# Two ends of the on-chip memory swapped, and y of the second MoE put on the weights' remainder

## The chip, the cores and the metric

One core of one Trainium2 chip runs the whole program. The metric is the device time of one execution in microseconds (us); the time before is the median of three runs.

## The reference

Inputs are q, k, v of shape (4, 8, 576, 64) and a decay f, and the weights of two pairs of dense layers. What is computed is

```python
scores = q @ k.T / sqrt(64) + decay(f)          # causal, per batch and head
x = softmax(scores) @ v                         # 2304 tokens x 512
x = leaky(x @ w_in) @ w_out                     # first MoE,  512 -> 2048 -> 512
out = ((x @ w_a) * (x @ w_b)) @ w_out2          # second MoE, 512 -> 1536 -> 512
```

All three parts run in full float32 accuracy: an operand is split into a high and a low part of type float32r, and each product is made of three matmuls (high by high, high by low, low by high).

## The kernel before, in words

The program is one function, scheduled by a list scheduler in the order in which it is written; it places the waits itself. TensorE does all products. A matmul has a stationary operand (first loaded as weights, 128 x 128) and a moving operand, which streams past it; in the profile `ab<-yh,wa_hi` means that the moving yh met the stationary wa_hi.

- **Attention** goes in eight blocks (`att_steps`, L642), all its tiles in the pool `att` (L136). P is transposed by TensorE against the identity: the identity moves (it lies in `cpool`), p is stationary.
- **First MoE**: nine chunks of 256 tokens (i) by sixteen slices of the hidden width (fi). `work` (L688) issues `l1` (L529: 12 matmuls L537, stationary w_in, moving x, 256 columns) and, two or three steps later, `l2` (L551: 12 matmuls L559, stationary w_out, moving gh and gl, 256 columns). x, hs, gh and gl lie in the pool `moe_a` (L130), every third x in `late` (L718). Raw weights come through the pool `stage` (L132), go by ScalarE, VectorE and GpSimd into float32r (`load_weight`, L105) and stay in `wpool` (L58), 64 tiles of 2048 bytes per partition. Attention blocks are interleaved up to chunk 6. y goes to device memory (L569).
- **Second MoE**: five blocks n of 512 tokens (the last has 256) by twelve slices fi. `l3` (L598) issues 24 matmuls L608 (stationary w_a, w_b; moving yh, yl; 512 columns, in the last block 256), and `l4` (L622) issues for each of 4 groups of tokens (2 in the last block) 3 matmuls L631 (stationary ph or pl, moving w_out2, 512 columns). `load_y` (L587) brings y back and splits it, for block 0 before and for block n + 1 at fi = 4 of block n: the y of even blocks lies in the pool `wx`, that of odd blocks in `wk` (L589). `wx` (L733) also holds ph, pl, the raw weights and eight weight tiles: both parts of w_a, w_b and w_out2 of fi = 0 and of w_a of fi = 1 (L581); the other weights take over `wpool`, tile by tile, as the first MoE lets go of them. `wx` opens when `att` has closed, `wk` when `moe_a` has closed (L745 to L747).

A pool is a stretch of each partition. Pools are stacked from the bottom upwards, or, with side="right", from the top (byte 229344) downwards. A place is told here by its first byte in the partition; it follows from the pools' sizes, in the order in which they open. In the kernel before:

```
cpool   1152 ..   2240     identity at 1152
wpool   2240 .. 133312     64 weight tiles of 2048
moe_a 133312 .. 158912     xh, xl, hs, gh, gl      (later wk, 133312 .. 153792: yh, yl, os)
stage 158912 .. 172224     raw weights             (later late, 158912 .. 167104: xh, xl)
att   172704 .. 229344     attention               (later wx, 167904 .. 229344: 8 weight tiles,
                           raw, yh at 200672, yl at 208864, p, ph and pl from 221152)
```

All these tiles are multiples of 64 bytes long but for some small ones of attention, which lie at multiples of 32, so the remainder of a tile's place by 64 is mostly that of its pool: 0 for cpool's identity, wpool, moe_a, wk, stage and late, 32 for att and wx. By 512 it is 192 for wpool, moe_a and wk, and 480 for wx's weights, y, ph and pl.

Of the kernel before, what the change touches and what calls it, by code (L numbers as in the profile page):

```python
# [9 lines left out]
F32R = mybir.dt.float32r  # L10
# [4 lines left out]
PSUM = bass.MemoryType.PSUM  # L15
DRAM = bass.MemoryType.DRAM

P = 128
# [8 lines left out]
def kernel(  # L27
# [19 lines left out]
    NF1, NF2, ND = F1 // P, F2 // P, DM // P  # L47
# [37 lines left out]
    def split(hi, lo, src, lo_engine=None):  # L85

        nc.scalar.copy(hi, src)  # L87
        (lo_engine or nc.gpsimd).tensor_tensor(out=lo, in0=src, in1=f32(hi), op=ALU.subtract)
# [38 lines left out]


    moe_ctx = ExitStack()
    mp = moe_ctx.enter_context(tc.tile_pool(name="moe_a", bufs=2))  # L130
    stage_ctx = ExitStack()
    stage = stage_ctx.enter_context(tc.tile_pool(name="stage", bufs=2))  # L132
    late = {}
    ps_y = moe_ctx.enter_context(tc.tile_pool(name="ps_y", bufs=2, space=PSUM))
    att_ctx = ExitStack()
    ap_ = att_ctx.enter_context(tc.tile_pool(name="att", bufs=1, side="right"))  # L136
    ps_a = att_ctx.enter_context(tc.tile_pool(name="ps_att", bufs=1, space=PSUM, side="right"))


# [10 lines left out]
    for t in range(5):  # L150
        n = min(P, S - t * P)
# [357 lines left out]
    def att_tail(b):  # L509

        tok0 = b * S + 512
        c = tok0 // T1
        c0 = tok0 - c * T1
        ch, cl = x_chunk(c)
        pp = ps_a.tile([P, HP, 64], F32, tag="ps", bufs=3, name=f"ppx_{b}")
        for hp in range(HP):
            pe_att.transpose(pp[:, hp, :], x4[b][0:64, hp, :], ident[:64, :64])
        evac(ch[:, :, c0 : c0 + 64], cl[:, :, c0 : c0 + 64], pp)
# [53 lines left out]
    T2 = 512  # L572
    blocks2 = [(t, min(T2, NT - t)) for t in range(0, NT, T2)]
    wb = {}
    right = ExitStack()
    pools = {}

    def load_b(fi):
# [8 lines left out]
    def load_y(n):  # L587
        t0, tn = blocks2[n]
        pool = pools["wk" if n % 2 else "wx"]  # L589
        yh = pool.tile([P, ND, T2], F32R, tag="yh", bufs=1, name=f"yh_{n}")  # L590
        yl = pool.tile([P, ND, T2], F32R, tag="yl", bufs=1, name=f"yl_{n}")
        for d in range(ND):
            t = pools["wx"].tile([P, T2], F32, tag="t", bufs=2, name=f"sy_{n}_{d}")[:, :tn]
            nc.sync.dma_start(t, y_dram[d, :, t0 : t0 + tn])
            split(yh[:, d, :tn], yl[:, d, :tn], t, nc.vector if n == 0 else None)
        yb[n] = (yh, yl)
# [118 lines left out]
    for item in one[:8]:  # L715
        work(*item)
    stage_ctx.close()
    late["p"] = moe_ctx.enter_context(tc.tile_pool(name="late", bufs=1))  # L718
    att_tail(0)
    for _ in att_steps(2):  # L720
        pass
# [8 lines left out]
                if i % 2 == 0:  # L730
                    att_tail(i // 2)
    att_ctx.close()
    pools["wx"] = right.enter_context(tc.tile_pool(name="wx", bufs=2, side="right"))  # L733
    pools["ps_ab"] = right.enter_context(tc.tile_pool(name="ps_ab", bufs=2, space=PSUM, side="right"))

    for fi in range(NF1):
        for i in (NB1 - 2, NB1 - 1):
            work(i, fi)
        if fi == 11:
            load_y(0)  # L740
        while len(wb) < NF2 and 4 * fi >= 6 * (len(wb) + 1) - 8:
            load_b(len(wb))
# [1 line left out]
        l2(*pend.pop(0))  # L744
    moe_ctx.close()  # L745
    wk_ctx = ExitStack()
    pools["wk"] = wk_ctx.enter_context(tc.tile_pool(name="wk", bufs=2))  # L747
    pools["ps_o"] = wk_ctx.enter_context(tc.tile_pool(name="ps_o", bufs=4, space=PSUM))
    while len(wb) < NF2:
        load_b(len(wb))  # L750
# [1 line left out]
    for n in range(len(blocks2)):  # L752
        for fi in range(NF2):
            pend.append((n, fi, *l3(n, fi)))
            if fi == 4 and n + 1 < len(blocks2):
                load_y(n + 1)
            if len(pend) > 1:
                l4(*pend.pop(0))
    while pend:
        l4(*pend.pop(0))  # L760
    wk_ctx.close()
    right.close()


# [28 lines left out]
```

## Time and profile before

| what | value |
|---|---|
| median of 3 runs | 1154.49 us (1154.03 to 1155.28) |
| the profiled execution's own time | 1155.12 us |
| its span, first to last instruction | 1153.3 us |
| granted TensorE clock, mean | 0.995 |

The profile is of one execution. Its views used below are the page (busy time of engines, the chain that ended last, DMA issues), the busy time by stretches of the span, the chain of waits in order of time (each piece: start, length, what it is, and how many instructions were merged; the length of a piece of matmuls divided by their count is the spacing from one matmul's start to the next), the timeline of an engine, and SyncE's waits. A matmul's own duration in the trace is a latency and not the spacing: matmuls overlap.

### The profile page before, as it was taken

How to read it: one execution, taken by the hardware profiler on the slowest of the kernel's cores; microseconds unless marked ns; L12 is line 12 of the kernel's file. 1: busy time of each engine (PE TensorE's matmuls, PEld its weight loads, DVE VectorE, ACT ScalarE, POOL GpSimd, SP SyncE). 2: the span in 40 equal slices, each digit the busy share in tenths (PEclk: the TensorE clock that was granted, in tenths of full speed). 3: DMA queues.
4: the chain of work that ended last, by engine and by line, in shares of the span. 5: the costliest groups of instructions: out<-in, count | busy, mean ns of one | idle time of the engine just before them, and what ended most of it. 6: DMA issues, size and time to landing. Idle time of an engine off the chain costs nothing.

```text
span 1153.3 us, 20360 instructions
## 1 busy us (share of the span) xinstructions
PE 1112.6 (96%) x7021; PEld 981.9 (85%) x7021; DVE 658.0 (57%) x1780; ACT 571.8 (50%) x1511; POOL 286.8 (25%) x486
## 2 busy tenths in 40 slices
PE   6999989999999999999999899999999999999998
PEld 3677778999989999999999887888888888888897
DVE  6789998887878787866459978111111211211122
ACT  5557687888877777867445545212111211211121
POOL 5556553333233323322124324101000100100000
PEclk9999999999999999999999999999999999999999
DMA  7556645433353234521234444101000100100010
GB/s 195 162 150 171 149 121 107 91 79 63 66 122 77 55 69 95 104 51 30 88 115 129 149 143 145 40 1 55 19 1 1 64 1 1 39 8 1 1 37 19
DMA packets 188583, 86.82 MB, mean 75 GB/s; under 512 B 144640, under 2 KB 174336, under 8 KB 188480
## 3 DMA queue, kind: packets, MB, share of 16 engines
q1 hardware_dynamic: 183296, 80.80, 27.9%
q10 hardware_dynamic: 5184, 4.72, 1.2%
q8 instruction: 55, 0.90, 0.3%
q14 instruction: 48, 0.39, 0.1%
HBM read 75.96 MB, written 9.51 MB: 74 GB/s over the span
## 4 chain that ended last, share of the span: by engine, by line
PE 69%; DVE 5%; issue 4%; DMA 3%; ACT 2%; POOL 1%; SPq 0%; ACTq 0%; POOLq 0%; DVEq 0%
PE ab L608 25%; PE o L631 13%; PE h L537 11%; PE y L559 11%; PE av L76 3%; PE s L76 3%; PE pp L76 2%; DMA xk<-in_k_dram 1%; DVE gl L546 1%; DMA sy<-y_dram 1%; DMA y_dram<-yo 1%; DVE c_wc L97 0%; ACT p L283 0%; ACT gh L544 0%; DVE c_wb L97 0%
## 5 line engine op out<-in xcount | busy, mean ns | idle before, releaser
L614 DVE TENSOR_TENSOR p<-ab,p 128x512 f32<-128x512 f32 (+1 forms) x60 | 38.3, 639 | 302.6 <-PE ab L608 299.4
L537 PE MATMUL h<-xh,wi_hi 128*128 128x256 f32 x576 | 168.6, 293 | 8.7 <-ACT hs L545 8.6
L559 PE MATMUL y<-gl,wo_hi 128*128 128x256 f32 x576 | 161.6, 287 | 3.4 <-DVE gl L546 3.4
L537 PE MATMUL h<-xl,wi_hi 128*128 128x256 f32 x576 | 164.7, 286 | 0.0
L537 PE MATMUL h<-xh,wi_lo 128*128 128x256 f32 x576 | 164.6, 286 | 0.0
L559 PE MATMUL y<-gh,wo_lo 128*128 128x256 f32 x576 | 160.5, 285 | 0.0
L559 PE MATMUL y<-gh,wo_hi 128*128 128x256 f32 x576 | 154.4, 292 | 3.9 <-ACT gh L544 3.9
L613 ACT COPY p<-ab 128x512 f32<-128x512 f32 (+1 forms) x60 | 32.7, 545 | 186.3 <-PE ab L608 186.3
L537 PEld LDWEIGHTS h<-xh,wi_hi 128*128 128x128 f32 x576 | 111.2, 193 | 15.7 <-ACT hs L545 12.0
L559 PEld LDWEIGHTS y<-gl,wo_hi 128*128 128x128 f32 x576 | 110.5, 192 | 5.0 <-DVE gl L546 4.3
L305 POOL TENSOR_SCALAR p<-cumb,ncum_t 128x384 f32<-128x384 f32 (+1 forms) x112 | 70.4, 630 | 169.5 <-PE pp L76 41.7
L537 PEld LDWEIGHTS h<-xh,wi_lo 128*128 128x128 f32 x576 | 111.3, 193 | 1.2 <-issue 1.2
L537 PEld LDWEIGHTS h<-xl,wi_hi 128*128 128x128 f32 x576 | 111.5, 194 | 0.8 <-issue 0.4
L559 PEld LDWEIGHTS y<-gh,wo_hi 128*128 128x128 f32 x576 | 104.6, 191 | 7.6 <-ACT gh L544 5.7
L559 PEld LDWEIGHTS y<-gh,wo_lo 128*128 128x128 f32 x576 | 110.7, 192 | 0.4
L87 ACT CAST pph<-p 128x512 fp32r<-128x512 f32 (+1 forms) x60 | 34.7, 578 | 130.5 <-DVE p L614 130.4
L283 ACT ACTIVATE p<-p,stat 128x384 f32<-128x384 f32 (+4 forms) x128 | 77.3, 604 | 26.0 <-DVE stat L312 22.3
L608 PE MATMUL ab<-yh,wb_hi 128*128 128x512 f32 (+1 forms) x240 | 88.8, 370 | 0.7 <-ACT yo L568 0.7
L608 PE MATMUL ab<-yh,wb_lo 128*128 128x512 f32 (+1 forms) x240 | 88.9, 370 | 0.0
L608 PE MATMUL ab<-yl,wa_hi 128*128 128x512 f32 (+1 forms) x240 | 88.8, 370 | 0.0
L608 PE MATMUL ab<-yh,wa_hi 128*128 128x512 f32 (+1 forms) x240 | 88.8, 370 | 0.0
L608 PE MATMUL ab<-yl,wb_hi 128*128 128x512 f32 (+1 forms) x240 | 88.7, 370 | 0.0
(164 smaller groups left out, 2766.3 us busy)
## 6 DMA issues: line engine op xcount, KB each, us to landing
cumb<-cum_dram SPq DMA_DIRECT2D x32, 288.0 KB, 3.7
raw_wi<-in_moe_w_in_dram SPq DMA_DIRECT2D x32, 256.0 KB, 3.1
raw_wo<-in_moe_w_out_dram SPq DMA_DIRECT2D x32, 256.0 KB, 3.2
raw_wa<-in_moe_w_a_dram SPq DMA_DIRECT2D x12, 512.0 KB, 3.6
raw_wb<-in_moe_w_b_dram SPq DMA_DIRECT2D x12, 512.0 KB, 3.5
raw_wc<-in_moe_w_out_dram SPq DMA_DIRECT2D x12, 512.0 KB, 3.6
xq<-in_q_dram SPq DMA_DIRECT2D x144, 32.0 KB, 2.0
y_dram<-yo ACTq DMA_DIRECT2D x36, 128.0 KB, 2.7
```

The source lines that it names most:

```text
L76: return method(*args, **kw)
L87: nc.scalar.copy(hi, src)
L283: act_att.activation(pt, pt, AF.Exp, bias=stat[:, 0, s : s + 1], scale=-1.0, accum_out=stat[:, 1, s : s + 1])
L305: pool_att.tensor_scalar(pt, cumb[:, :n], 1.0, ncum_t[:, t, bh : bh + 1], op0=ALU.mult, op1=ALU.add)
L537: nc.tensor.matmul(hps, w[:, c * P : c * P + P], x[:, c, :], start=(n == 0), stop=(n == 3 * ND - 1))
L546: nc.vector.tensor_tensor(out=gl, in0=hs, in1=f32(gh), op=ALU.subtract)
L559: nc.tensor.matmul(o, w[:, d * P : d * P + P], g, start=(fi == 0 and n == 0 and d % 2 == 0), stop=(fi == NF1 - 1 and n == 2 and d % 2 == 1),)
L608: nc.tensor.matmul(o[:, :tn], w[:, c * P : c * P + P], y[:, c, :tn], start=(m == 0), stop=(m == 3 * ND - 1))
L613: nc.scalar.copy(p[:, :tn], ab[0][:, :tn])
L614: nc.vector.tensor_tensor(out=p[:, :tn], in0=ab[1][:, :tn], in1=p[:, :tn], op=ALU.mult)
L631: nc.tensor.matmul(o, g[:, t * P : t * P + P], w, start=(fi == 0 and m == 0), stop=(fi == NF2 - 1 and m == 2))
```

## The change

The pools moe_a, stage, late and wk go to the top of the memory, att and wx to the bottom, above wpool. yl of odd blocks is made 72 columns (288 bytes) longer than it is used, and the last block uses columns 8 to 263 of its y tiles in place of 0 to 255. The names of two context stacks change.

```diff
-    mp = moe_ctx.enter_context(tc.tile_pool(name="moe_a", bufs=2))
+    mp = moe_ctx.enter_context(tc.tile_pool(name="moe_a", bufs=2, side="right"))
     stage_ctx = ExitStack()
-    stage = stage_ctx.enter_context(tc.tile_pool(name="stage", bufs=2))
+    stage = stage_ctx.enter_context(tc.tile_pool(name="stage", bufs=2, side="right"))
...
-    ap_ = att_ctx.enter_context(tc.tile_pool(name="att", bufs=1, side="right"))
+    ap_ = att_ctx.enter_context(tc.tile_pool(name="att", bufs=1))
...
         yh = pool.tile([P, ND, T2], F32R, tag="yh", bufs=1, name=f"yh_{n}")
-        yl = pool.tile([P, ND, T2], F32R, tag="yl", bufs=1, name=f"yl_{n}")
+        yl = pool.tile([P, ND * T2 + 72 * (n % 2)], F32R, tag="yl", bufs=1, name=f"yl_{n}")[:, : ND * T2].rearrange("p (d t) -> p d t", d=ND)
+        if tn < T2:
+            yh, yl = yh[:, :, 8:], yl[:, :, 8:]
...
-    late["p"] = moe_ctx.enter_context(tc.tile_pool(name="late", bufs=1))
+    late["p"] = moe_ctx.enter_context(tc.tile_pool(name="late", bufs=1, side="right"))
...
-    pools["wx"] = right.enter_context(tc.tile_pool(name="wx", bufs=2, side="right"))
+    pools["wx"] = late_ctx.enter_context(tc.tile_pool(name="wx", bufs=2))
...
-    pools["wk"] = wk_ctx.enter_context(tc.tile_pool(name="wk", bufs=2))
+    pools["wk"] = wk_ctx.enter_context(tc.tile_pool(name="wk", bufs=2, side="right"))
```

## Rows read from the trace of the kernel before

**Rows 1.** The page: busy time of the engines, and the chain by engine and line.

```profile
PE 1112.6 (96%) x7021; PEld 981.9 (85%) x7021; DVE 658.0 (57%) x1780; ACT 571.8 (50%) x1511; POOL 286.8 (25%) x486
...
PE 69%; DVE 5%; issue 4%; DMA 3%; ACT 2%; POOL 1%; SPq 0%; ACTq 0%; POOLq 0%; DVEq 0%
```

**Rows 2.** Busy time by stretches: columns as the first line names them, x instructions.

```profile
core 0: us, PE busy (x) PEld busy (x) DVE busy (x) ACT busy (x) POOL busy (x), PEclk, DMA share, GB/s
...
64.00:190.00 126.00, 117.01 (x786) 96.11 (x786) 118.72 (x364) 90.44 (x269) 69.57 (x107) 0.99 0.55 141
190.00:598.00 408.00, 400.60 (x3259) 393.24 (x3258) 312.49 (x996) 303.80 (x854) 120.20 (x259) 1.00 0.37 81
598.00:697.00 99.00, 91.55 (x721) 88.50 (x719) 83.91 (x128) 51.62 (x117) 33.33 (x25) 0.98 0.44 134
697.00:1153.30 456.30, 451.94 (x2101) 372.56 (x2100) 99.73 (x152) 89.95 (x166) 28.81 (x23) 1.00 0.08 26
```

**Rows 3.** Chain in order of time, second MoE, blocks 1, 2 and 3.

```profile
814.11 5.47 PE ab L608 x24
819.59 2.79 PE o L631 x12
822.38 5.45 PE ab L608 x24
...
913.12 5.59 PE ab L608 x24
918.71 2.80 PE o L631 x12
921.52 5.60 PE ab L608 x24
...
1013.82 5.47 PE ab L608 x24
1019.29 2.79 PE o L631 x12
1022.09 5.45 PE ab L608 x24
```

**Rows 4.** Same view, the first two slices of block 1, then of block 2.

```profile
797.41 5.60 PE ab L608 x24
803.01 2.80 PE o L631 x12
805.81 5.55 PE ab L608 x24
811.36 2.75 PE o L631 x12
...
896.60 5.45 PE ab L608 x24
...
904.85 5.55 PE ab L608 x24
910.39 2.73 PE o L631 x12
```

**Rows 5.** Same view, block 4 (256 columns): its first two slices and two later.

```profile
1096.31 2.87 PE ab L608 x24
...
1101.97 2.83 PE ab L608 x24
...
1106.18 2.80 PE ab L608 x24
...
1110.38 2.80 PE ab L608 x24
```

**Rows 6.** Same view, first MoE between attention's pieces.

```profile
501.09 1.43 PE h L537 x12
502.52 1.20 PE y L559 x10
503.72 0.35 PE s L76 x2
504.07 0.77 PE pp L76 x7
```

**Rows 7.** Same view, shares of the stretches 190:598 and then 598:697 by line.

```profile
by line: PE y L559 27.0%; PE h L537 26.7%; PE av L76 9.8%; PE s L76 8.4%; PE pp L76 6.9%; issue 5.9%; DMA xk<-in_k_dram 2.9%; ACT p L283 1.1%; DVE gl L546 1.0%; DMA raw_wa<-in_moe_w_a_dram 0.9%; DMA y_dram<-yo 0.8%; ACT ph L354 0.7%; DVE pl
...
by line: issue 23.8%; PE h L537 14.7%; PE y L559 12.5%; DMA sy<-y_dram 7.9%; DVE gl L546 6.1%; DVE c_wc L97 4.1%; DVE c_wb L97 3.4%; DVE c_wc L95 2.5%; DVE c_wa L97 2.4%; ACT gh L544 2.3%; DVE c_wa L96 2.2%; DVE c_wa L100 2.0%; DVE c_wc L96
```

**Rows 8.** Timeline of TensorE, first attention blocks: transposes and a product.

```profile
107.51 0.71 PE L76 MATMUL pp<-ident,p 128*128 128x128 f32 x5
111.95 1.28 PE L76 MATMUL av<-vn,ph 128*128 128x128 f32 x10
```

**Rows 9.** Timeline of GpSimd: yl of block 1, then of block 2.

```profile
802.11 1.29 POOL L88 TENSOR_TENSOR yl<-sy,yh 128x512 fp32r<-128x512 f32 x1 [0.67 <-ACT yh L87]
...
899.27 1.29 POOL L88 TENSOR_TENSOR yl<-sy,yh 128x512 fp32r<-128x512 f32 x1 [1.70 <-ACT yh L87]
```

**Rows 10.** SyncE's waits: total us, times, longest us.

```profile
SPq L114 <- PE ppx L76: 39.5, 1, 39.5
```

**Rows 11.** The page, DMA issues: count, KB each, median us to landing.

```profile
cumb<-cum_dram SPq DMA_DIRECT2D x32, 288.0 KB, 3.7
raw_wi<-in_moe_w_in_dram SPq DMA_DIRECT2D x32, 256.0 KB, 3.1
raw_wo<-in_moe_w_out_dram SPq DMA_DIRECT2D x32, 256.0 KB, 3.2
raw_wa<-in_moe_w_a_dram SPq DMA_DIRECT2D x12, 512.0 KB, 3.6
```

More of the change, by code (lines that the diff above doesn't have):

```diff
@@ L574 @@
     wb = {}
-    right = ExitStack()
+    late_ctx = ExitStack()
     pools = {}
@@ L732 @@
     att_ctx.close()
-    pools["wx"] = right.enter_context(tc.tile_pool(name="wx", bufs=2, side="right"))
-    pools["ps_ab"] = right.enter_context(tc.tile_pool(name="ps_ab", bufs=2, space=PSUM, side="right"))
+    pools["wx"] = late_ctx.enter_context(tc.tile_pool(name="wx", bufs=2))
+    pools["ps_ab"] = late_ctx.enter_context(tc.tile_pool(name="ps_ab", bufs=2, space=PSUM, side="right"))
     for fi in range(NF1):
@@ L761 @@
     wk_ctx.close()
-    right.close()
+    late_ctx.close()
 _INS = ['q', 'k', 'v', 'f', 'moe_w_in', 'moe_w_out', 'moe2_w_a', 'moe2_w_b', 'moe2_w_out']
```

## The prediction

> **What bounds the kernel now.** I read the busy times first: TensorE is busy for 96% of the span, no other engine for more than 57%, and the chain that ended last consists of TensorE for 69% [rows 1]. By stretches [rows 2]: up to 190 us VectorE is as busy as TensorE (118.72 and 117.01 of 126 us); from 190 to 598 us, where the first MoE and attention share TensorE, it has 400.60 of 408 us; from 598 to 697 us, where chunks 7 and 8 run while the weights of the second MoE are converted, 91.55 of 99 us; in the second MoE it waits for nothing. The granted clock is 1.00, that is 2.4 GHz, but for short low stretches. So the time is the sum of the matmuls' spacings, and I read those from the chain. The reader is to see that one and the same loop runs at two speeds. A group of 24 matmuls L608 takes 5.45 to 5.47 us in blocks 1 and 3 and 5.59 to 5.60 us in block 2 [rows 3]: 227 against 233 ns each. Blocks 1 and 3 have their y in wk (remainder 0 by 64, as the weights in wpool), block 2 in wx (remainder 32). The first slices turn it round [rows 4]: there the weights lie in wx too, and the group takes 5.60 us in block 1 (y at 0, weights at 32) and 5.45 us in block 2 (both at 32); at fi = 1, where half of the weights lie in wx, both take 5.55. So neither pool is slow by itself: with 512 columns, **equal remainders give 227 ns and unequal ones 233**. L631 fits: ph and pl (32) against w_out2 (0) take 2.79 to 2.80 us for 12 [rows 3], and 2.73 to 2.75 where w_out2 lies in wx as well [rows 4]. With 256 columns it is the other way [rows 5]: 2.87 us for 24 with both at 32, 2.83 for the half and half slice, 2.80 with y at 32 and weights at 0, so equal ones give 119.6 ns and **unequal ones 116.7**. The first MoE (256 columns, x, gh, gl and weights all at 0) has 1.43 us for 12, or 119.2 ns, and 1.20 for 10 [rows 6]: the slow case.
>
> **Where the change puts things.** Nothing is added, removed or reordered but places. att and wx begin at 133312: remainder 0; in wx yh then lies at 166080 and ph at 186560, both 0 by 64 and 192 by 512. moe_a begins at 229344 - 25600 = 203744, late at 195552, stage at 190432: all 32 by 64. wk, with 8192 + 8480 + 4096 = 20768 bytes, begins at 208576: 0 by 64 and 192 by 512, as the weights (without the 288 extra bytes it would be 32). Block 4's y, 8 columns further on, is at 32 again. So:
> - all 512-column matmuls of the second MoE get equal remainders;
> - those of block 4's L608 stay, or become, unequal;
> - all of the first MoE's become unequal;
> - attention's pairs inside att keep their relation, but the transposes (identity at 0, p formerly at 32) become equal.
>
> **Second MoE, part by part.** All of it lies on the path.
> 1. L608 in blocks 0 and 2: 10.5 groups each at 5.60 that become 5.45: 21 x 0.15 = 3.15 us.
> 2. L608 in the first two slices of blocks 1 and 3: (0.15 + 0.10) x 2 = 0.5 us.
> 3. Block 4's first two slices: 0.07 + 0.03 = 0.1 us.
> 4. L631: 4 x 12 + 6 = 54 groups of 12, less 4.5 that have it already, from 2.79 to 2.73 (12 x 227 ns): 49.5 x 0.06 = 3.0 us; with 2.75 it is 2.0.
>
> Sum 6.75 us.
>
> **First MoE.** 1.43 us for 12 becomes 12 x 116.7 ns = 1.40, or 2.1%. What counts is what lies on the path: L537 and L559 hold 53.7% of the chain from 190 to 598 us, that is 219 us, and 27.2% of 99 us after it [rows 7]: 4.6 + 0.6 us. Before 190 us, where VectorE is as long, I take 0.3 us of the 1.0 that 384 matmuls could give. Sum 5.5 us. The bounds: nothing, if the wait for another engine ends each stretch at the same time anyway (from 598 us on ScalarE, VectorE and GpSimd convert weights and the chain is 23.8% issue and much VectorE [rows 7]); at most 3456 x 2.9 ns (the larger difference, of [rows 5]) = 10 us. I am near the middle, by the chain.
>
> **Transposes.** Now 0.77 us for 7, 110 ns [rows 6]. No row shows one with equal remainders. The nearest is a product of attention's first blocks, whose operands both lie in att: 1.28 us for 10 beside 0.71 us for 5 transposes [rows 8]. Each piece ends with the latency of its last matmul; taking 110 ns for the transposes it is 0.27 us, and the product has 112 ns. So transposes may lose 2 ns of 110. They hold 6.9% of 408 us on the chain [rows 7]: 28 us, 0.5 us lost. Bounds: a gain of 0.7 if they fared as the 512 columns (6 of 233 ns), and a loss of 2.3 if they rose to the 119 ns of 256 columns.
>
> **At nothing.** The elementwise engines don't see the remainder: GpSimd takes 1.29 us to write yl in block 1 (at 0) and in block 2 (at 32) [rows 9], so what they do in the moved pools keeps its time; should it not, the cover is TensorE, as they are idle for most of the second MoE [rows 2]. Waits: wx still takes over what att leaves, wk what moe_a leaves, late what stage leaves. The first raw weight of the second MoE waits for attention's last transpose [rows 10] and will still do so; behind it in SyncE's queue stand only the other raw weights. The pad is never read.
>
> **Sum.** 6.75 + 5.5 - 0.5 = 11.75 us off the profiled execution's own 1155.12: 1143.4. That execution lies 0.6 us above the median of the runs, so **1142.7 us** against 1154.49.
>
> **The rivals.**
> - *The first MoE gives nothing.* Either its spacing is not ruled as block 4's (other engines were quiet there), or other waits take up what the matmuls leave. For it: from 190 to 598 us TensorE's lines hold 79% of the chain and not all of it, and from 598 us the chain goes through VectorE and ScalarE [rows 7]. Against it: TensorE is busy for 400.60 of 408 us [rows 2]. Time: 1155.1 - 6.75 + 0.5 - 0.6 = 1148.2.
> - *Place has no effect; the two speeds have another cause.* Then the change does not do what it says, and the time is 1154.5. Against it: the switch at fi = 0 and fi = 1 in both directions [rows 4]. The Trainium skill's page "SBUF — State Buffer", section "Who interferes with whom", speaks for it: TensorE has two independent read ports, one for the moving operand and one for loading weights, and never waits for anyone. By that rule the sum would be 0; no row agrees with it here.
> - *The region, not the remainder.* All unequal pairs of before also have one operand below 153792 and one above 167904 [rows 3, 4]. If that is what counts, blocks 1 and 3 (y now at 208576) lose 21 x 0.15 = 3.15 us, blocks 0 and 2 gain nothing (y at 166080, taken as above), L631 neither, and the first MoE, now far apart, gains its 5.5: 1154.5 + 3.15 - 5.5 = 1152.1, the edge of what can be told. Against it: one remainder explains as much without a border that no row shows.
> - *Slower: loads land later at remainder 32.* The 64 raw weights of the first MoE land in stage, now at 0, then at 32. For it: cumb, in att at 32, takes 3.7 us for 288 KB, raw_wi at 0 takes 3.1 for 256 KB [rows 11]. Against it: raw_wa, at 32, takes 3.6 us for 512 KB. If each were 0.4 us later and each on the path up to 190 us, 25.6 us are lost and the time is 1168. It decides from 11.75 / 64 = 0.18 us a load; five raw buffers stand between the loads and the conversion.
>
> **How the numbers follow.** Forecast 0.73; first MoE gives nothing 0.13; region 0.05; no effect 0.04; loads 0.05. The lower end of the range: 6.75 + 10 with no loss on transposes gives 1137.7, and one low-clock stretch less (2% of 99 us from 598 us on [rows 2]) up to 2 us more: 1136.5. The upper end takes in the first rival with a transposes' loss a little larger: 1149. What can be told from no change is 0.2%, 2.3 us. Faster by more: 0.73 + 0.13 + half of the region case = 0.88; the same: 0.07; slower: 0.05.
>
> **What would show it.** Right: groups of 24 L608 at 5.45 us in every block and slice up to block 3, 2.80 us in all of block 4; groups of 12 L631 at 2.73; 12 L537 at 1.40; the second MoE 6.75 us shorter than 456.30. Each step can fail alone: blocks 1 and 3 at 5.60 would mean region; everything at old spacings, no effect; 1.40 with an unchanged stretch from 190 to 598 us, the first rival; seven transposes at 0.83 in place of 0.77, the larger loss; raw_wi landing in over 3.3 us, the loads. The forecast is wrong if block 4 or the first MoE asks for a difference of 288 bytes by 512 (as block 4 has now) and not just of 32: block 4, then at 224 by 512 against 192, would show it.

## The result, and the profile after

The changed kernel takes 1144.89 us in the median of its first four runs, against 1154.26 for the kernel before; the ratio of its runs is 0.9905, with an interval from 0.9881 to 0.9930, which is 11.0 us of 1154.26 (8.1 to 13.7). One of the four, the profiled one, fell at about half the granted clock (0.56, 1772.74 us); it is left out of the ratio (the other three have 1143.48 in the middle), and all lines of "after" below come from a second profile of the same kernel, whose own time is 1144.92 us at a span of 1143.1. In that second set the ratio was 0.9901 (0.9882 to 0.9919). The forecast was 1142.7 us, in a range of 1136.5 to 1149.0.

The lines of the code have moved: L608 is now L610 and L631 is L633; L537 and L559 stay. Busy time of the engines, from the page after (answers to [rows 1]):

```profile
PE 1099.7 (96%) x7021; PEld 976.3 (85%) x7021; DVE 658.1 (58%) x1780; ACT 570.4 (50%) x1511; POOL 287.0 (25%) x486
```

The counts are those of before, and each engine runs the same instructions in the same order. TensorE is busy for 12.9 us less, the weight loads for 5.6 us less, and no other engine moves by more than 1.4 us. So all that changed is how long TensorE's instructions take. The stretches after, with the columns of [rows 2]; the second MoE begins at 694.9 us here and at 697.0 before:

```profile
190.00:598.00 408.00, 398.99 (x3274) 391.78 (x3274) 312.62 (x997) 304.77 (x858) 121.09 (x261) 0.99 0.36 80
598.00:694.90 96.90, 88.14 (x714) 84.49 (x712) 83.58 (x128) 50.61 (x115) 33.27 (x25) 1.00 0.44 136
694.90:1143.10 448.20, 443.98 (x2102) 372.52 (x2100) 100.98 (x152) 89.66 (x166) 28.35 (x23) 1.00 0.08 26
```

The second MoE gave 456.30 - 448.20 = 8.1 us, all that lies ahead of it only 2.1 us. The chain in order of time (start, length, what) shows the 8.1 us. Block 1 after, from its first slice on, against [rows 3, 4]:

```profile
792.66 5.44 PE ab L610 x24
...
800.82 5.44 PE ab L610 x24
806.26 2.72 PE o L633 x12
...
817.14 5.44 PE ab L610 x24
```

Block 2 after, its second and fourth slice, the same view:

```profile
898.74 5.44 PE ab L610 x24
...
915.06 5.44 PE ab L610 x24
920.50 2.72 PE o L633 x12
```

Block 4 after, its first two slices and a later one, the same view, against [rows 5]:

```profile
1086.42 2.80 PE ab L610 x24
...
1091.96 2.80 PE ab L610 x24
...
1100.34 2.80 PE ab L610 x24
```

One loop now runs at one speed: 5.44 us in block 2, where it took 5.60, and 5.44 in block 1, where it took 5.45 to 5.47; 2.72 in place of 2.79 to 2.80 for the 12 matmuls of the second product; the slow first slices (5.60, 5.55) are gone too, and block 4 begins at 2.80 and not at 2.87. The loads, which one rival wanted later, land as before or earlier [rows 11]; from the page after (count, KB each, median us to landing):

```profile
raw_wi<-in_moe_w_in_dram SPq DMA_DIRECT2D x32, 256.0 KB, 3.1
raw_wo<-in_moe_w_out_dram SPq DMA_DIRECT2D x32, 256.0 KB, 3.0
```

What is left to explain: which part of the edit does it, and why a first MoE with a smaller spacing on 3456 matmuls hardly starts the second one sooner.

### The profile page after: what moved, and what is told of

It is laid out like the page before. It is cut to its first block, busy times and chain, and to the rows that moved or that the text cites. A ratio compares the mean times of both kernels' runs of the same rounds, so it can differ in the third digit from the quotient of the medians.

```text
span 1770.9 us, 20360 instructions
## 1 busy us (share of the span) xinstructions
PE 1754.6 (99%) x7021; PEld 1380.1 (78%) x7021; DVE 656.7 (37%) x1780; ACT 578.8 (33%) x1511; POOL 280.1 (16%) x486
## 4 chain that ended last, share of the span: by engine, by line
PE 98%; DMA 1%; DVE 0%; ACT 0%; SPq 0%; issue 0%; DVEq 0%; ACTq 0%
PE ab L610 28%; PE h L537 19%; PE y L559 19%; PE o L633 14%; PE s L76 7%; PE av L76 6%; PE pp L76 4%; PE tk L76 0%; DMA raw_wo<-in_moe_w_out_dram 0%; DMA cum_dram<-cum 0%; PE tq L76 0%; PE px L76 0%; PE ppx L76 0%; DMA fs<-in_f_dram 0%; DVE c_wi L100 0%; SPq L275 0%
## 5 line engine op out<-in xcount | busy, mean ns | idle before, releaser
L537 PE MATMUL h<-xh,wi_hi 128*128 128x256 f32 x576 | 223.6, 388 | 0.0
L537 PE MATMUL h<-xh,wi_lo 128*128 128x256 f32 x576 | 221.2, 384 | 0.0
L537 PE MATMUL h<-xl,wi_hi 128*128 128x256 f32 x576 | 221.2, 384 | 0.0
L559 PE MATMUL y<-gl,wo_hi 128*128 128x256 f32 x576 | 220.7, 386 | 0.0
L559 PE MATMUL y<-gh,wo_lo 128*128 128x256 f32 x576 | 219.2, 383 | 0.0
L559 PE MATMUL y<-gh,wo_hi 128*128 128x256 f32 x576 | 210.8, 393 | 0.1
L537 PEld LDWEIGHTS h<-xh,wi_hi 128*128 128x128 f32 x576 | 161.0, 279 | 7.2 <-issue 3.9
L537 PEld LDWEIGHTS h<-xh,wi_lo 128*128 128x128 f32 x576 | 164.3, 285 | 2.7 <-POOL p L306 1.4
L537 PEld LDWEIGHTS h<-xl,wi_hi 128*128 128x128 f32 x576 | 163.3, 284 | 2.2 <-issue 1.1
L559 PEld LDWEIGHTS y<-gl,wo_hi 128*128 128x128 f32 x576 | 163.0, 283 | 2.2 <-issue 0.8
L559 PEld LDWEIGHTS y<-gh,wo_lo 128*128 128x128 f32 x576 | 162.6, 282 | 1.8 <-issue 0.2
L559 PEld LDWEIGHTS y<-gh,wo_hi 128*128 128x128 f32 x576 | 152.6, 273 | 5.8 <-issue 1.3
L544 ACT ACTIVATE gh<-h 128x256 fp32r<-128x256 f32 x144 | 55.3, 384 | 246.0 <-PE h L537 175.2
L610 PE MATMUL ab<-yh,wa_hi 128*128 128x512 f32 (+1 forms) x240 | 129.5, 539 | 0.0
L610 PE MATMUL ab<-yh,wb_lo 128*128 128x512 f32 (+1 forms) x240 | 129.2, 538 | 0.0
L610 PE MATMUL ab<-yl,wb_hi 128*128 128x512 f32 (+1 forms) x240 | 129.0, 538 | 0.0
L610 PE MATMUL ab<-yh,wa_lo 128*128 128x512 f32 (+1 forms) x240 | 128.9, 537 | 0.0
L610 PE MATMUL ab<-yh,wb_hi 128*128 128x512 f32 (+1 forms) x240 | 128.8, 537 | 0.0
L610 PE MATMUL ab<-yl,wa_hi 128*128 128x512 f32 (+1 forms) x240 | 128.4, 535 | 0.0
```

The costliest lines, as they stand in the source:

```text
L537: nc.tensor.matmul(hps, w[:, c * P : c * P + P], x[:, c, :], start=(n == 0), stop=(n == 3 * ND - 1))
L544: nc.scalar.activation(gh, hps, AF.Prelu, alpha=0.01)
L559: nc.tensor.matmul(o, w[:, d * P : d * P + P], g, start=(fi == 0 and n == 0 and d % 2 == 0), stop=(fi == NF1 - 1 and n == 2 and d % 2 == 1),)
L610: nc.tensor.matmul(o[:, :tn], w[:, c * P : c * P + P], y[:, c, :tn], start=(m == 0), stop=(m == 3 * ND - 1))
```

## The experiments

### The change again, and one half at a time

The change again, unaltered:

> The changed kernel as it is, for a trace at the full granted clock. By remainder: groups of 24 matmuls of l3 at 5.45 us in every slice of blocks 0 to 3 and 2.80 in block 4; 12 matmuls of l4 at 2.73; 12 of l1 at 1.40; the second MoE 6.75 us shorter, the first 4 to 6, the time 1142.7 us. If the first MoE gives nothing: 1.40 for 12, but the stretch up to 697 us as long as before and the time near 1148. By region: blocks 1 and 3 at 5.60 and the time near 1152.

Measured: the 1144.14 us in the median (1139.52 to 1146.58) and the lines above.

The first MoE's half alone: 32 bytes are put ahead of the first MoE's pools in the kernel before, and nothing else moves.

```diff
     moe_ctx = ExitStack()
+    moe_ctx.enter_context(tc.tile_pool(name="pad", bufs=1)).tile([P, 8], F32, tag="pad", name="pad")
```

> The kernel before with 32 bytes left free below the pool of the first MoE while that pool is open: x, gh and gl go from remainder 0 to 32, y of odd blocks, attention, and all of the second MoE stay where they were; no region changes. By remainder: 12 matmuls of l1 at 1.40 us in place of 1.43, the second MoE as before (5.60 in even blocks, 5.45 in odd ones), the time 5.5 us shorter, 1148.8. By region: no difference anywhere, 1154.3. If the first MoE gives nothing: 1.40 for 12 but 1154.3.

Measured: 1153.62 us, ratio 0.9987 (0.9973 to 1.0000). The chain of this kernel in the first MoE, against [rows 6]:

```profile
501.19 1.40 PE h L538 x12
502.59 1.17 PE y L560 x10
```

and in block 2 of the second MoE, which this edit doesn't touch:

```profile
911.64 5.59 PE ab L609 x24
917.23 2.80 PE o L632 x12
```

The second MoE's half alone: the same 32 bytes lie on the other side, under attention's pool and wx, and block 4 gets the change's shift.

```diff
+    ctx.enter_context(tc.tile_pool(name="pad", bufs=1, side="right")).tile([P, 8], F32, tag="pad", name="pad")
...
+        if tn < T2:
+            yh, yl = yh[:, :, 8:], yl[:, :, 8:]
```

> The kernel before with 32 bytes left free at the top of the memory, and block 4's columns 8 on: attention and the pool of the even blocks' y, of ph, pl and of the early weights go from remainder 32 to 0, the first MoE and y of odd blocks stay; no region changes. By remainder: 24 matmuls of l3 at 5.45 us in all blocks up to 3, block 4 at 2.80, 12 of l4 at 2.73, 12 of l1 still 1.43, transposes between 0.77 and 0.83 for 7; the time 6.75 us shorter, up to 0.5 given back by the transposes: 1148.0. By region: no difference, 1154.3.

Measured: 1145.24 us, ratio 0.9920 (0.9906 to 0.9934). The chain of this kernel, first in the first MoE, then in block 2 and in block 4:

```profile
503.13 1.44 PE h L538 x12
504.57 1.20 PE y L560 x10
...
506.12 0.77 PE pp L76 x7
...
917.94 5.44 PE ab L611 x24
923.38 2.72 PE o L634 x12
...
1103.22 2.80 PE ab L611 x24
```

The two halves come apart cleanly. Places alone switch the spacing, without any swap of ends, so "place has no effect" is refuted. The Trainium skill's page "SBUF — State Buffer", section "Who interferes with whom", gives TensorE two independent read ports, and says that TensorE never waits for anyone. By the prediction's reading of that rule places would be worth nothing; here 24 matmuls take 5.44 or 5.60 us by where their two operands begin relative to each other, and the measurement decides. What in the reading or loading makes the difference, no run here shows. "Region" falls too: a shift of 32 bytes within the same region does all that the move across the memory does. The two ratios make 1.5 + 9.2 = 10.7 us of 1154.94, the whole change 11.4: the halves add up, and the first MoE's is the small one. Its spacing fell exactly as forecast (1.40 for 12, 1.17 for 10) and yet the kernel gained 1.5 us and not 5.5. The transposes, which have equal remainders here, still take 0.77 us for 7.

Both halves at once, still without the swap: the two edits above in one kernel.

> The kernel before with both gaps of 32 bytes (below the first MoE's pool, and at the top) and block 4's columns from 8 on, no ends swapped: the remainders by 256 are those of the changed kernel in every pair. By remainder: as the changed kernel, 1144. By region, or if the swap itself does something: nearer to 1154.

Measured: 1143.43 us, ratio 0.9906 (0.9885 to 0.9927), as the change itself. Swapping the ends is thus only a way to set remainders.

### By which length the remainder counts

In the changed kernel, yh of blocks 0 to 4 begins 16, 32, 48, 64 and 16 bytes later, and g of chunks 2, 3 and 4 is taken 16, 32 and 48 bytes further on in its tiles. The longer tiles put more at other places: yl, behind a longer yh, lies 64 bytes further still (80, 96, 112, 128 and 80 bytes off), ph 128 bytes, and the first MoE's pool, now 384 bytes longer, begins 384 bytes lower.

```diff
+        k = (0, 0, 4, 8, 12, 0, 0, 0, 0)[i]
+        gh = mp.tile([P, T1 + 16], F32R, tag="gh", bufs=3, name=f"gh_{i}_{fi}")[:, k : k + T1]
...
+        k = (4, 8, 12, 16, 4)[n]
+        yh = pool.tile([P, ND * T2 + 16], F32R, tag="yh", bufs=1, name=f"yh_{n}")
```

> The changed kernel with y 16, 32, 48 and 64 bytes further on in blocks 0 to 3, 16 in block 4, and gh and gl 16, 32 and 48 bytes further on in chunks 2, 3 and 4 of the first MoE. By remainder with a period of 64: block 1 at 5.60 us for 24, block 3 at 5.45, blocks 0 and 2 between the two or beyond; 12 matmuls of l2 at 1.44 in chunk 3 (equal remainders), 1.40 in the others, those at 16 and 48 unknown. If the period is longer than 64, block 3 is slow too, and l4 too, whose ph now lies 128 bytes off its remainder by 512. By region: all blocks alike.

Measured: 1157.27 us, one run. The chain of this kernel in blocks 0, 1, 2 and 3 (yh 16, 32, 48 and 64 bytes off), then in block 4 (16):

```profile
730.24 5.57 PE ab L611 x24
...
830.51 5.58 PE ab L611 x24
836.09 2.80 PE o L634 x12
...
914.24 5.59 PE ab L611 x24
...
1022.98 5.57 PE ab L611 x24
1028.55 2.79 PE o L634 x12
...
1112.28 2.84 PE ab L611 x24
```

Block 3, with yh 64 and yl 128 bytes off, should have been fast if the remainder by 64 counted; it is as slow as block 1. The second product, with ph 128 bytes off, is slow as well, so the length is over 128. Block 4 takes 2.84 us, between the 2.80 and 2.87 of [rows 5]. In chunks 2 to 4 the shifted g made no difference that could be told (117 to 119 ns a matmul), but nothing follows from that: the whole pool of the first MoE had moved, and `l1`, whose x was not shifted in its tiles, takes 1.41 to 1.43 us here and not the 1.40 of the change.

The next kernel tells 256 from 512: the changed kernel with 8 extra columns in place of 72 (y in blocks 1 and 3 moves by 64 x 4 = 256 bytes), and block 4 without its shift.

```diff
-        yl = pool.tile([P, ND * T2 + 72 * (n % 2)], F32R, tag="yl", bufs=1, name=f"yl_{n}")[:, : ND * T2].rearrange("p (d t) -> p d t", d=ND)
-        if tn < T2:
-            yh, yl = yh[:, :, 8:], yl[:, :, 8:]
+        yl = pool.tile([P, ND * T2 + 8 * (n % 2)], F32R, tag="yl", bufs=1, name=f"yl_{n}")[:, : ND * T2].rearrange("p (d t) -> p d t", d=ND)
```

> The changed kernel with yl of odd blocks 8 columns longer in place of 72 (their y then has 448 by 512 and 192 by 256, the weights 192 by both), and block 4's y from column 0 (equal remainders). If the remainder by 256 decides: blocks 1 and 3 at 5.45 us for 24 as with 72 columns, block 4 at 2.87 in place of 2.80, in all 0.8 us more for the second MoE. If by 512: blocks 1 and 3 at 5.60.

Measured: 1145.66 us, one run. The chain of this kernel in block 1 and in block 4:

```profile
817.00 5.44 PE ab L608 x24
822.44 2.72 PE o L631 x12
...
1096.16 2.87 PE ab L608 x24
1100.42 2.87 PE ab L608 x24
```

Moved by 256 bytes, block 1 stays fast, as did block 2 in the kernel with the second half alone, where y and ph are 256 bytes apart from the weights by 512. So **the remainder by 256** counts for 512 columns: 0 is fast, and all the differences tried (16, 32, 48 and 64 bytes for yh, 80 to 128 for yl, 128 for ph) are slow. Block 4 at equal remainders takes 2.87 and not 2.80: with 256 columns the relation is the other way round, as read from [rows 5]. By which length it goes there is not shown: 32 and 288 bytes of difference give 2.80, 0 gives 2.87, and 16 with 80 gives 2.84.

### What takes the first MoE's gain

The start of the second MoE tells how much of the first one's gain arrives. It is the first time in these lines (a tile's instructions: shortest, median and longest duration in ns, then the first and the last start), here of the kernel with the first half alone, of the one with the second half alone, and of the one with both:

```profile
L609 PE MATMUL ab<-yh,wa_hi x240: 277/392/398, 695.4 to 1143.4; 128*128 128x512 f32 x96, 128*128 128x256 f32 x24
```

```profile
L611 PE MATMUL ab<-yh,wa_hi x240: 277/389/397, 697.7 to 1137.6; 128*128 128x512 f32 x96, 128*128 128x256 f32 x24
```

```profile
L612 PE MATMUL ab<-yh,wa_hi x240: 277/389/401, 689.0 to 1128.9; 128*128 128x512 f32 x96, 128*128 128x256 f32 x24
```

With the first MoE at its old places it starts at 697.0 and 697.7, with the new places at 695.4 and 694.9 (the change): some 2 us sooner. But the third kernel starts at 689.0, 8.0 us sooner than before, with the same spacing. Its run was the fastest of its six (1139.09 us). The waits of TensorE from 190 to 598 us (line waited for, total us, times, longest us) name where to look. After:

```profile
PE s L76 <- DVE stat L312: 4.2, 3, 1.8
```

Before, in the first and then in a second trace of the same kernel:

```profile
PE s L76 <- DVE stat L312: 2.3, 4, 0.8
```

```profile
PE s L76 <- DVE stat L312: 4.0, 3, 1.8
```

At the first score of each of attention's later batches TensorE waits for VectorE, which holds on for xk's load (1.5 us of it at 327 us after, 1.6 before). That these waits grow with the change, as the first pair suggests, is not shown: the kernel before has the longer ones too, in its second trace. What follows one of them, in the timeline of TensorE after (start, length, what, idle before it):

```profile
329.35 0.44 PE L76 MATMUL s<-ks,qhh 128*128 128x384 f32 x1 [1.82 <-DVE stat L312]
...
330.76 0.28 PE L537 MATMUL h<-xh,wi_lo 128*128 128x256 f32 x1
330.88 0.35 PE L537 MATMUL h<-xh,wi_hi 128*128 128x256 f32 x1
331.02 0.42 PE L537 MATMUL h<-xl,wi_hi 128*128 128x256 f32 x1
331.24 0.42 PE L537 MATMUL h<-xh,wi_lo 128*128 128x256 f32 x1
```

Some 1.5 us after the wait the spacing goes from 0.12 to 0.21 us, which is the lower level, 1.2 GHz. By stretches (columns of [rows 2], the granted clock third from last):

```profile
330.90:334.30 3.40, 3.40 (x17) 3.21 (x16) 2.05 (x11) 2.59 (x9) 0.35 (x2) 0.51 0.72 189
```

Such a stretch lasts some 3.4 us and would cost about 1.7, an estimate that takes TensorE to be the bound all through it. Stretches of 20 us show which kernel has one where. Before, at 320 and at 450 us:

```profile
320.00:340.00 20.00, 17.92 (x125) 16.53 (x124) 14.83 (x55) 16.01 (x52) 6.86 (x15) 0.91 0.62 135
450.00:470.00 20.00, 18.82 (x150) 18.11 (x149) 15.12 (x55) 14.61 (x46) 8.29 (x17) 1.00 0.60 114
```

After:

```profile
320.00:340.00 20.00, 16.91 (x118) 15.62 (x117) 14.01 (x54) 15.51 (x50) 6.59 (x14) 0.91 0.61 134
450.00:470.00 20.00, 18.07 (x135) 17.38 (x135) 14.48 (x54) 13.65 (x44) 6.43 (x15) 0.91 0.57 115
```

The kernel with both paddings, the fast one:

```profile
320.00:340.00 20.00, 17.53 (x138) 16.50 (x137) 16.59 (x57) 15.79 (x49) 7.70 (x17) 1.00 0.59 136
450.00:470.00 20.00, 17.34 (x135) 16.16 (x134) 16.07 (x53) 15.33 (x47) 7.78 (x14) 1.00 0.53 113
```

0.91 is one low stretch in 20 us. Counted so from 64 us to the start of the second MoE, before has 3, after 4, the first half alone 5, and the fast one 2 (in one piece of 6.8 us), none of them behind 190 us. That one waits too (3.3 us in three such waits, the longest 1.5) without a fall; nor did the clock fall after a wait of 1.6 us at 671 us in the trace after. Ahead of the low stretch of before at 326 us, on the other hand, lie three waits of 0.3 to 0.5 us. So idle time is what precedes a low stretch, not what is enough for it.

The next three kernels try to fill these waits: 4, 8 and 5 extra matmuls of 512 columns, whose result is overwritten, stand ahead of that first score in batches 1 to 3; in the kernel before, with the first half, and in the changed kernel.

```diff
+            if b and (r, h, i) == (1, 0, 0):
+                for _ in range((0, 4, 8, 5)[b]):
+                    pe_att.matmul(sp, qhh[:, :P], wa[0][0], start=True, stop=True)
```

> The kernel before with 4, 8 and 5 extra matmuls of 512 columns (TensorE's product of q with first-MoE weights, into the bank that the first score of batches 1, 2 and 3 overwrites) just ahead of those scores, where TensorE sat idle in the traces. Theory low clock: the low-clock stretch at 326 us goes or stays, at most one fewer, so 1.7 us off, less what of the 17 x 0.23 = 3.9 us of extra matmuls is not idle time: 1153 to 1157. Its use is as the base for the next two, which have the same order of instructions.

> The same extra matmuls with 32 bytes free below the first MoE's pool. Theory low clock (the first MoE's gain was given back by low-clock stretches after idle time of TensorE): without those idle times there are no more low stretches here than in the kernel before with the extra matmuls, and the gain over it is 4 to 5.5 us. Theory other waits (other engines end each stretch at the same time anyway): the gain stays at 1 to 1.5 us, as without the extra matmuls.

> The changed kernel with the same extra matmuls. Low clock: 8.1 us for the second MoE and 4 to 5.5 for the first below the kernel before with them, about 1141 us, and faster than the changed kernel without. Other waits: about 10 us below the kernel before with them, no faster than the changed kernel.

Measured: 1158.96 (ratio 1.0037, 1.0024 to 1.0051), 1154.96 (1.0005, 0.9994 to 1.0016) and 1146.46 us (0.9932, 0.9911 to 0.9953). The fillers mostly didn't fall into the waits: other work was reordered around them, and before lost 4.3 us by 17 matmuls that at 227 ns take 3.9. But within this set the first half is worth 1.0037 - 1.0005 = 3.2 per mille, 3.7 us, more than the 1.5 without fillers, and the kernel with fillers and the first half shows one low stretch only, that with fillers alone two. With some 2 us of noise on either side of the 3.7 this doesn't decide between the two theories. As a remedy the fillers are a miss: the changed kernel with them is no faster than without (0.9932 against 0.9901; the intervals overlap).

Another try at the same wait: the changed kernel with the loads of cumb in batches 1 to 3 issued by GpSimd, so that xk's loads stand sooner in SyncE's queue.

```diff
-            nc.sync.dma_start(cumb[:, :nk], cum_dram[bh : bh + 1, :nk].to_broadcast([P, nk]))
+            (nc.gpsimd if b else nc.sync).dma_start(cumb[:, :nk], cum_dram[bh : bh + 1, :nk].to_broadcast([P, nk]))
```

> The changed kernel with the loads of cumb for batches 1 to 3 issued by GpSimd, which also frees their buffers, in place of SyncE, whose queue held the loads of q and k behind them. If the low-clock stretches at 331 and 460 us come from TensorE's idle time there, and that from the loads of k: both go, and the time is 3 us or more below the changed kernel's 1144. If GpSimd's issues are dear or the idle time has another source: 1144 or more.

Measured: 1149.61 us (1144.38 to 1154.03), ratio 0.9949 (0.9931 to 0.9967): slower than the change by some 5 us, with other work reordered, a low stretch still at 453 us and longer waits. A miss as well.

Last, the kernel before and the first half alone once more, each for a second trace:

> The kernel before once more, for a second trace. Low clock: the second MoE begins 692 us after the start plus 1.7 us for every low-clock stretch of 3.4 us between 64 us and there (before: 697.0 with three; the kernel with the gap at the top alone: 697.7 with three). Other waits: the start does not go with the number of stretches.

> The kernel before with 32 bytes free below the first MoE's pool, once more. Low clock: the second MoE begins at 687 us plus 1.7 us a stretch (the first trace: 695.4 with five), about 5 us earlier than before at the same number of stretches, while the median of the runs is again only 1 to 4 us shorter if it meets more of them. Other waits: 1 to 2 us earlier whatever the number.

Measured: the kernel before started its second MoE at 696.8 us, with 2 low stretches, 1.4 us later than its expectation. The first half took 1154.40 us (1152.74 to 1155.99), ratio 0.9978 (0.9966 to 0.9990), or 2.5 us, and started it at 696.4 with 3 low stretches, some 4 us later than that expectation said. If a stretch costs 1.7 us, the starts without them are 691.9, 693.4 and 692.6 us for three traces at the old places, and 686.9, 691.3, 688.1, 685.6 and 686.2 at the new ones (the first half twice, the change, both paddings, the 8 columns). The mean difference is 5.0 us, near the forecast 5.5, but one of the five hardly shows it, and the first chunk's stretch alone varies between some 114 and 117 us from trace to trace.

The same eight traces also split into TensorE's busy and idle time. From 64 us to the start of the second MoE, with the columns of [rows 2], before, in the second trace of before, and after:

```profile
64.00:697.00 633.00, 609.17 (x4760) 577.86 (x4759) 515.12 (x1487) 445.86 (x1238) 223.10 (x391) 0.99 0.42 101
```

```profile
64.00:696.80 632.80, 608.36 (x4760) 576.31 (x4759) 514.53 (x1487) 445.38 (x1239) 223.37 (x391) 0.99 0.42 101
```

```profile
64.00:694.90 630.90, 604.53 (x4760) 572.26 (x4759) 514.30 (x1487) 445.18 (x1238) 223.53 (x391) 0.99 0.41 101
```

The length less TensorE's busy time is its idle time: 23.8, 24.4 and 22.2 us at the old places, and 26.9, 25.9, 26.4, 25.3 and 26.4 at the new ones, in the order of above. On average the busy time falls by 5.8 us, the idle time grows by 2.7, and the second MoE starts 3.1 sooner. The growth is clearest from 598 us on, where weights are converted: 7.4, 7.0 and 6.8 us of idle time at the old places, 8.5, 7.9, 8.8, 8.2 and 8.6 at the new ones; from 190 to 598 us the two sets overlap (7.4 to 8.9 and 8.4 to 9.8). The new places also meet 3.8 low stretches against 2.7, which at 1.7 us each is 1.9 us of busy time. So the matmuls became some 7.7 us shorter; **waits took 2.7 us of that back, in every trace at the new places, and the clock perhaps another 1.9**. The clock's share stays open. The granted clock of every run points the same way: leaving aside runs below 0.99, it is 0.9952 on average over the 18 runs of the first half and 0.9966 over the 48 of the kernel before, which is one low stretch more. But among these 48 a lower clock does not go with a longer time, so the 1.7 us a stretch is not borne out there.

None of the kernels tried beats the changed one: that with both paddings equals it.

## Why the prediction was right, and where its terms were off

Right in sign and in mechanism: places alone set the spacing, and each loop went to the speed that was worked out. That the sum came out so near, 11.75 us forecast against 11.0 and 11.4 measured, is in part luck: two terms gave more than forecast and one much less.

- **Second MoE, terms 1 to 4: undersized.** 6.75 us forecast, 8.1 measured. Each block and slice did what the step said, but the groups go to 5.44 and 2.72 us and not to 5.45 and 2.73, and 226.7 to 227.2 ns stand against 233.1 to 233.3 on average over the loops. By the spacings of the whole stretch the first product gave 4.3 us (3.75 forecast), the second 3.7 (3.0). The blocks counted as fast before still lost a little ([rows 3] has 5.47 beside 5.45), and the 2.79 that the second product was read at hides 2.80. A hundredth of a microsecond in each of some 100 groups is no longer small.
- **Transposes: no loss.** 0.5 us forecast; at equal remainders 7 of them take 0.77 us as before. The step took a difference of 2 ns from two pieces of different length [rows 8]; that was no difference of spacing.
- **First MoE: the spacing right, the gain oversized.** 1.43 became 1.40 as worked out, but of the 5.5 us between 1.5 and 2.5 arrived (ratios 0.9987 and 0.9978, a start 2.1 us sooner in the trace after). The step that failed is that a share of the chain was turned into a saving: it says which work is on the path now, not what TensorE will meet when it comes sooner. In the traces 2.7 us went into idle time; the prediction named such waits as a bound and in a rival, but gave the sum no term for them. It had the clock only at the lower end of its range, as one low stretch less; the new places met about one more, whose price is not settled. The first rival ("the first MoE gives nothing", 1148.2) had named the right place, and the range took it in.
- **Which remainder counts: by 256, not by 64.** The text listed the remainders by 64 and by 512. It gave the right answer only because all pairs of the two MoEs in both kernels stand 0 or 32 bytes apart by 256, and 64 divides 256. It did name the case to look for: block 4 with 32 bytes of difference (after) and with 288 (before) are equally fast.
- **Rivals.** No effect: refuted by the halves. Region: refuted, the 32 bytes alone do it. Later loads: not seen, 3.1 and 3.0 us after, 3.1 and 3.2 before.

## What to carry to other kernels

When one loop runs at two speeds in one profile, list where its operands begin before looking for another cause: here, with fp32r matmuls of 512 columns, moving and stationary operand at the same remainder by 256 bytes are worth 2.7% of a TensorE-bound stretch, with 256 columns 32 bytes of difference are worth 2.3%, and 32 bytes of padding buy either. A saving on the bounding engine counts in full only where that engine waits for nothing; where it meets another engine regularly, ask what it will wait for when it comes sooner. And take a second trace of the kernel before: the longer waits that a single pair of traces laid to the change stood in it too.

## What the runs showed of the hardware that was not expected

- The relation of two places sets TensorE's spacing, and its sign turns with the number of columns: 512 columns 227 ns (equal by 256 bytes) against 233, 256 columns 119.5 (equal) against 116.7 to 117.0 (32 or 288 bytes apart), 128-column transposes 109 either way.
- A wait of 1.8 us in a stretch that is otherwise full was followed by some 3.4 us at 1.2 GHz, after the work had gone on at 2.4 GHz for about 1.5 us; waits of up to 1.5 us in another run of the same work, and one of 2.4 us at 326 us in the kernel whose cumb is loaded by GpSimd, were followed by none.
- A long low stretch at the start cost nothing that can be seen. The fast run with both paddings had a mean granted clock of 0.78 in its first 64 us:

```profile
0.00:64.00 64.00, 51.26 (x166) 31.46 (x167) 43.97 (x145) 36.71 (x112) 35.26 (x74) 0.78 0.65 178
```

TensorE is busy there for 51.26 of 64 us and the second MoE began sooner than in any other trace; low stretches were therefore counted from 64 us on. The runs agree: 21 of the 69 of the kernel before have a mean granted clock of 0.979 to 0.985, which such a stretch would give, and they took 1155.1 us on average, the other 48 (0.994 to 0.999) 1155.3.
